# Block-sparse attention and a token mix on one core: edge queries in twelve joined units, two places for the keys, and key copies spread over three engines

## The chip, the cores and the metric

The kernel runs on one core of one Trainium2 chip. The metric is the device time of one execution in microseconds (us). Before the change it was 636.45 us, the median of three runs from 635.98 to 636.53. All parts of the profile below are of one profiled execution, which took 636.82 us; the span from its first to its last instruction was 635.0 us, so 1.8 us lie around the span.

The engines are called as the profile calls them: PE multiplies matrices (PEld loads its stationary operand), DVE is the vector engine, ACT the scalar engine, POOL is GpSimd, and SP issues most of the DMAs. PSUM is the memory that PE writes to, SBUF the main on-chip memory.

## The reference

A block-sparse attention over 4 batches, 8 heads, 768 tokens and 64 channels per head feeds a token mix. Blocks have 32 tokens, so there are 24 of them. A query block sees its own block and the two beside it, the first and the last block, and three sampled blocks; the first and the last query block see everything.

```python
mask = np.abs(blk_i - blk_j) <= window            # window = 1
mask = mask | (blk_i == 0) | (blk_j == 0) | (blk_i == n_blocks - 1) | (blk_j == n_blocks - 1)
for qb in range(n_blocks):
    for kb in sampled_blocks[qb]:
        mask[qb*block:(qb+1)*block, kb*block:(kb+1)*block] = True
scores = np.where(mask, scale * q @ k.T, -1e9)
attn = np.exp(scores - np.max(scores, -1, keepdims=True))
x = (attn / (attn.sum(-1, keepdims=True) + 1e-9)) @ v       # then (batch, 768, 512)

theta = x @ w_theta
y = w_tok_r @ (x * cos(theta)) + w_tok_i @ (x * sin(theta)) # over the tokens
u = x + y
out = u + np.maximum(u @ w_ch, 0.0)
```

The four weights come as 64-bit floats. The kernel decodes them from their two 32-bit words into a high and a low part, and multiplies with both.

## The kernel before

Two stages follow each other: `attention` and `token_mix`. Both run on the same engines, and the last steps of the first overlap the first loads of the second.

**Attention** works on two pairs of batches, one after the other. A pair has 30 units: 8 wide units (the two edge query blocks, once for each batch and half of the heads, against all 768 keys; tiles SW, PW, Tw, XW) and 22 inner units (query blocks 1 to 22 for all heads, against 8 key blocks gathered into a buffer kg). A unit passes through five steps on different engines: scores on PE into a PSUM tile S, the row extremes m on DVE (TENSOR_REDUCE, L291), the exponentials P on ACT (L300, four instructions), eight transposes on PE and their copy from PSUM to pT on ACT (L307, L309), the products with the values on PE (L318, tile X), and the division by the row sums on DVE (L325 to L328), whose result xo is stored to the intermediate xs in HBM. The order is written out by hand: step n of the loop in `attention` issues the scores of unit n+1, the transposes of unit n, the weights of unit n+1 and the values of unit n-1, and around them the work that prepares later units.

That preparation is what the change touches. `gather_k` fills kg for unit n+2 from the pair's keys kb: window and edge blocks on ACT with a scaling of -1/8 (L235), three sampled blocks on DVE at addresses held in registers (L244), which `number_blocks` loads (L224, TENSOR_LOAD). There is one buffer for kb, so the keys of the second pair can be loaded only when the first pair has been gathered (L209). `load_window` loads the neighbouring value rows into one of two buffers va (L260, L263); `gather_v` fetches the sampled value rows into one of three buffers vb with an indirect DMA from POOL's queue (L270). The `Decoder` decodes one third of a piece of 512 weight columns in most steps: `bits` (L67 to L69), `rest` (L75, L77) and `low` (L83, L84) on DVE, `start` and `high` (L63, L80) on ACT. A new raw piece is loaded when `low` has freed its buffer.

**The token mix** runs 48 steps. In each PE computes an angle block (tile h, L517 to L519) and 24 products into y (L555 to L557), later also the output products o (L578 to L580). The last weight, w_ch, is decoded in its first 12 steps, two thirds of a 256-column piece in a step.

Of the kernel before, what the change touches and what calls it, by code (L numbers as in the profile page):

```python
# [19 lines left out]
P = 128  # L20
# [3 lines left out]
VB_BUFS = 3  # L24
Q_AHEAD = 4
Q_BUFS = 3
RAW_AHEAD = 6
# [18 lines left out]
class Piece:  # L46
# [5 lines left out]
    def __init__(self, nc, hi, lo, src, name):  # L52
        self.nc, self.hi, self.lo, self.src, self.name = nc, hi, lo, src, name
        self.f = src.shape[1] // 2
# [10 lines left out]
    def bits(self):  # L65
        nc, a, ai = self.nc, self.a, self.a.bitcast(I32)
        nc.vector.tensor_scalar(a, a, WORD_LO, WORD_HI, op0=ALU.max, op1=ALU.min)  # L67
        nc.vector.tensor_scalar(ai, ai, 4, 1, op0=ALU.logical_shift_left, op1=ALU.logical_shift_right)
        nc.vector.scalar_tensor_tensor(ai, self.raw[:, :, 1], SIGN_BIT, ai, op0=ALU.bitwise_and, op1=ALU.bitwise_or)  # L69
# [12 lines left out]
    def low(self):  # L82
        self.nc.vector.tensor_tensor(self.a, self.a, self.hi.bitcast(F32), op=ALU.subtract)  # L83
        self.nc.vector.tensor_tensor(self.lo, self.a, self.raw[:, :, 0].bitcast(F32), op=ALU.add)  # L84


class Decoder:


    def __init__(self, pieces, pool, queue):  # L90
        self.pieces, self.pool, self.queue = pieces, pool, queue
        self.at = 0
        for piece in pieces[:2]:
            piece.load(pool, queue)

    def left(self):
        return max(3 * len(self.pieces) - self.at, 0)

    def ahead(self, n):

        for k in range(self.at, min(self.at + n, 3 * len(self.pieces))):
            piece = self.pieces[k // 3]
            if k % 3 == 0:
                piece.start()
            elif k % 3 == 2:
                piece.high()

    def go(self, n):
        for k in range(self.at, min(self.at + n, 3 * len(self.pieces))):
            piece = self.pieces[k // 3]  # L110
            (piece.bits, piece.rest, piece.low)[k % 3]()
            if k % 3 == 2 and k // 3 + 2 < len(self.pieces):
                self.pieces[k // 3 + 2].load(self.pool, self.queue)
        self.at += n
# [51 lines left out]
def attention(tc, qT, qE, kT, vr, sampled, xs, ident, pieces, follow):  # L166
# [9 lines left out]
    with ExitStack() as ctx, ExitStack() as early:  # L176
# [5 lines left out]
        vp = ctx.enter_context(tc.tile_pool(name="vp", bufs=2))  # L182
# [4 lines left out]
        ps_t = ctx.enter_context(tc.tile_pool(name="ps_t", bufs=1, space=PSUM))  # L187
        ps_x = ctx.enter_context(tc.tile_pool(name="ps_x", bufs=2, space=PSUM))
# [6 lines left out]
        vas = [cp.tile([P, 1040], F32, name=f"va{x}") for x in range(2)]  # L195
        vbs = [cp.tile([P, 1040], F32, name=f"vb{x}") for x in range(VB_BUFS)]
        kbs, qbs, qes, vws, st, xws, numbers = {}, {}, {}, {}, {}, {}, {}
# [8 lines left out]
        def load_k(bp, b, p0=0, n=4, queue=nc.sync):  # L206
            if (b, p0) == (0, 0):
                kbs[bp] = kp.tile([P, 8, NB, 32], F32, tag="kb", name=f"kb{bp}")
            queue.dma_start(kbs[bp][:, 4 * b + p0 : 4 * b + p0 + n], kT[bp, b][:, p0 : p0 + n])  # L209

        def load_edges(bp):
            raw = ep.tile([P, 512], F32, tag="qw", name=f"qw{bp}")
            nc.sync.dma_start(raw, qE[bp])
            qes[bp] = raw

        def turn_edges(bp):
            t = ep.tile([P, 2, 2, 4, 32], F32, tag="qe", name=f"qe{bp}")
            nc.vector.tensor_scalar(t.rearrange("r z b p f -> r (z b p f)"), qes[bp], -0.125, None, op0=ALU.mult)
            qes[bp] = t

        def number_blocks(bp, i):
            _, numbers[bp, i] = nc.values_load_multi_w_load_instructions(  # L224
                tab.block[0:1, 3 * i : 3 * i + 3], engines=[mybir.EngineType.DVE], min_val=0, max_val=NB - 1,
                skip_runtime_bounds_check_because="Tables clamps the block numbers",
            )

        def gather_k(bp, i):
            kg, kb = kgs[i % 2], kbs[bp]  # L230
            def blocks(b0, n):
                return kb[:, :, b0 : b0 + n, :].rearrange("r g s f -> r s g f")

            def copy(s0, b0, n):
                nc.scalar.activation(kg[:, s0 : s0 + n], blocks(b0, n), AF.Copy, scale=-0.125)  # L235

            if i <= 2:
                copy(3, 0, 1)
                copy(7, NB - 1, 1)
            for b0, n in fresh(i, i <= 2):  # L240
                copy(b0 % 3, b0, n)
            for k, number in enumerate(numbers.pop((bp, i))):
                src = kb[:, :, bass.ds(number, 1), :].rearrange("r g s f -> r s g f")
                nc.vector.tensor_scalar(kg[:, 4 + k : 5 + k], src, -0.125, None, op0=ALU.mult)  # L244
            st[bp, i] = dict(kg=kg)

        def fresh(i, new):

            runs = []
            for blk in range(i - 1 if new else i, i + 2):  # L250
# [5 lines left out]

        def load_window(bp, i):
# [3 lines left out]
            for b0, n in fresh(i, i <= 2):  # L261
                s0 = 32 * (b0 % 3)
                nc.sync.dma_start(va[s0 : s0 + 32 * n], vr[768 * bp + 32 * b0 : 768 * bp + 32 * (b0 + n)])  # L263
            st[bp, i]["va"] = va

        def gather_v(bp, i):
            vb = vbs[i % VB_BUFS]
            if i <= VB_BUFS:
# [7 lines left out]
            st[bp, i]["vb"] = vb  # L276

        def scores(bp, i):

            s = st[bp, i]  # L280
            q = qbs.pop((bp, i))
            kg = s["kg"]
            sc = ps_s.tile([P, 2, 2, 256], F32, tag="S", name=f"S{bp}_{i}")
            for b in range(2):
                for p in range(4):
                    for e in range(2):
                        rows = slice(64 * e, 64 * e + 64)
                        nc.tensor.matmul(sc[32 * p : 32 * p + 32, e, b, :], q[rows, b, p, :], kg[rows, :, 4 * b + p, :], start=True, stop=True)  # L288
            m = wp.tile([P, 2, 2], F32, tag="m", name=f"m{bp}_{i}", bufs=3)
            for e in range(2):  # L290
                nc.vector.tensor_reduce(m[:, e], sc[:, e], axis=AX.X, op=ALU.min)  # L291
            s["S"] = sc, m

        def weights(bp, i):
            s = st[bp, i]
            sc, m = s.pop("S")
            s["P"] = pt = wp.tile([P, 2, 2, 256], F32, tag="P", name=f"P{bp}_{i}")
            for e in range(2):
                for b in range(2):
                    nc.scalar.activation(pt[:, e, b, :], sc[:, e, b, :], AF.Exp, bias=m[:, e, b : b + 1], scale=-1.0)  # L300

        def turned(pts, name):

            n = len(pts)
            t = ps_t.tile([P, 8, 128], F32, tag="T", name=f"T{name}")
            for k, pt in enumerate(pts):
                nc.tensor.transpose(t[:, k, :], pt, ident)  # L307
            out = wp.tile([P, 8, 128], F32, tag="pT", name=f"pT{name}")
            nc.scalar.copy(out[:, :n], t[:, :n])  # L309
            return out  # L310
# [404 lines left out]
```

## Time and profile before

| what | value |
|---|---|
| median of 3 runs | 636.45 us |
| profiled execution, its span | 636.82 us, 635.0 us |
| PE, DVE, ACT, POOL busy | 89%, 73%, 57%, 7% of the span |
| DMA moved | 96.5 MB, 152 GB/s over the span |
| mean granted PE clock | 0.964 |

Busy shares are means over both stages. The stages differ: while attention runs (until about 290 us) DVE, PE and the DMA engines are each busy for 75 to 90% of the time, and in the token mix PE is busy nearly throughout and the DMA engines for a quarter. The parts of the profile that the prediction shows are not repeated here.

### The profile page before, as it was taken

Reading aid. Unit: us, or ns where it says so; the run is one execution under the profiler, and the core shown is the slowest. Engines: PE = TensorE matmul, PEld = TensorE weight load, DVE = VectorE, ACT = ScalarE, POOL = GpSimd, SP = SyncE. Lnnn points to the kernel's source line nnn. Section 1 sums busy time; section 2 is a strip of 40 time slices with the busy share of each in tenths; the row PEclk is TensorE's granted clock in tenths of the full one; section 3 lists DMA queues with packets and bytes.
Section 4 is the critical chain, followed back from the end, with each engine's and each line's share of the span. In section 5 each row is a group of like instructions: output and inputs, shape, how many; then the busy total and the mean of one; then the engine's idle time right before and its main releaser. Section 6 shows DMA issues by size and latency. Waiting matters only on the chain.

```text
span 635.0 us, 19148 instructions
## 1 busy us (share of the span) xinstructions
PE 563.2 (89%) x7808; PEld 483.1 (76%) x7808; DVE 463.5 (73%) x1239; ACT 361.0 (57%) x774; POOL 45.6 (7%) x56
## 2 busy tenths in 40 slices
PE   4987778769887768668999999999999999999997
PEld 1555545545455546547999999999999999999997
DVE  1897978875798878758999697575973767746554
ACT  1586768764587767656667564355642465524520
POOL 0101212211002211110000000000000000000000
PEclk9998989988898999887999999999999999999999
DMA  8859979999778997866542224211241211211002
GB/s 287 259 156 246 275 209 259 258 278 345 219 204 244 251 257 226 221 161 170 139 130 73 64 84 143 69 47 50 80 124 59 70 51 42 80 59 61 27 1 99
DMA packets 79959, 96.52 MB, mean 152 GB/s; under 512 B 5312, under 2 KB 64832, under 8 KB 79488
## 3 DMA queue, kind: packets, MB, share of 16 engines
q1 hardware_dynamic: 73088, 72.99, 39.2%
q0 software_dynamic: 4928, 17.57, 10.7%
q10 hardware_dynamic: 1856, 4.74, 2.1%
q8 instruction: 61, 1.00, 0.7%
q14 instruction: 26, 0.21, 0.1%
HBM read 82.70 MB, written 12.58 MB: 150 GB/s over the span
## 4 chain that ended last, share of the span: by engine, by line
PE 66%; DMA 18%; DVE 8%; issue 4%; ACT 2%; SPq 1%; DVEq 1%; ACTq 0%
PE y L555 10%; PE y L556 10%; PE y L557 10%; DMA va<-in_vr_dram 10%; PE X L318 4%; PE S L288 4%; PE T L307 4%; PE h L519 3%; PE h L518 3%; PE o L578 3%; PE h L517 3%; PE o L580 3%; PE o L579 3%; DMA kb<-in_kT_dram 3%; PE SW L357 2%
## 5 line engine op out<-in xcount | busy, mean ns | idle before, releaser
L300 ACT ACTIVATE P<-S,m 128x256 f32<-128x256 f32 x176 | 69.0, 477 | 15.1 <-DVE m L291 14.9
L307 PEld LDWEIGHTS T<-ident,P 128*128 128x128 f32 x352 | 42.1, 150 | 38.2 <-ACT P L300 25.9
L307 PE MATMUL T<-ident,P 128*128 128x128 f32 x352 | 60.5, 304 | 11.2 <-ACT P L300 6.1
L318 PE MATMUL X<-va,pT 128*32 128x65 f32 (+1 forms) x1408 | 50.3, 233 | 21.9 <-DMA va<-in_vr_dram 18.1
L291 DVE TENSOR_REDUCE m<-S 128x2 f32<-128x512 f32 x88 | 56.7, 686 | 16.7 <-PE S L288 9.8
L309 ACT COPY pT<-T 128x1024 f32<-128x1024 f32 x44 | 44.8, 1018 | 41.5 <-PE T L307 41.4
L288 PE MATMUL S<-kg,q 64*32 64x256 f32 x1408 | 55.1, 404 | 10.9 <-issue 10.9
L555 PE MATMUL y<-w_tok_r_hi,zh 128*128 128x384 f32 x192 | 64.6, 336 | 0.0
L556 PE MATMUL y<-w_tok_r_lo,zh 128*128 128x384 f32 x192 | 64.4, 335 | 0.0
L557 PE MATMUL y<-w_tok_r_hi,zl 128*128 128x384 f32 x192 | 64.3, 335 | 0.0
L556 PE MATMUL y<-w_tok_i_lo,zh 128*128 128x384 f32 x192 | 64.2, 334 | 0.0
L555 PE MATMUL y<-w_tok_i_hi,zh 128*128 128x384 f32 x192 | 64.2, 334 | 0.0
L557 PE MATMUL y<-w_tok_i_hi,zl 128*128 128x384 f32 x192 | 62.7, 334 | 0.0
L270 POOL DMA_INDIRECT vb<-in_vr_dram,rows x44 | 44.1, 1002 | 229.3 <-PE X L318 206.0
L318 PEld LDWEIGHTS X<-va,pT 128*32 128x32 f32 (+1 forms) x1408 | 35.6, 116 | 31.8 <-DMA va<-in_vr_dram 17.8
L517 PE MATMUL h<-w_theta_hi,xTh 128*128 128x256 f32 x192 | 55.8, 290 | 1.9 <-ACT xTh L508 1.9
L519 PE MATMUL h<-w_theta_hi,xTl 128*128 128x256 f32 x192 | 55.6, 290 | 0.5 <-DVE xTl L509 0.5
L518 PE MATMUL h<-w_theta_lo,xTh 128*128 128x256 f32 x192 | 55.3, 288 | 0.0
L318 PE MATMUL X<-vb,pT 128*32 128x65 f32 (+1 forms) x1408 | 49.8, 232 | 5.0 <-issue 5.0
L521 ACT ACTIVATE t<-h,up_int 128x256 f32<-128x256 f32 x48 | 22.7, 473 | 42.7 <-PE h L519 42.0
L528 ACT ACTIVATE cs<-rr 128x256 f32<-128x256 f32 x48 | 20.0, 416 | 45.8 <-DVE rr L526 45.8
L578 PE MATMUL o<-uh,w_ch_hi 128*128 128x384 f32 x128 | 42.5, 336 | 0.9 <-DVE of L584 0.9
(125 smaller groups left out, 1337.2 us busy)
## 6 DMA issues: line engine op xcount, KB each, us to landing
xa<-xs SPq DMA_DIRECT2D x192, 64.0 KB
va<-in_vr_dram SPq DMA_DIRECT2D x30, 260.0 KB
xr<-xs SPq DMA_DIRECT2D x24, 256.0 KB
out_dram<-of SPq DMA_DIRECT2D x32, 192.0 KB
q<-in_qT_dram SPq DMA_DIRECT2D x22, 256.0 KB
xs<-xo SPq DMA_DIRECT2D x44, 128.0 KB
vw<-in_vr_dram SPq DMA_DIRECT2D x6, 780.0 KB
raw_tok_r<-in_w_tok_r_dram SPq DMA_DIRECT2D x9, 512.0 KB
```

Source lines behind the costliest of these rows:

```text
L288: nc.tensor.matmul(sc[32 * p : 32 * p + 32, e, b, :], q[rows, b, p, :], kg[rows, :, 4 * b + p, :], start=True, stop=True)
L291: nc.vector.tensor_reduce(m[:, e], sc[:, e], axis=AX.X, op=ALU.min)
L300: nc.scalar.activation(pt[:, e, b, :], sc[:, e, b, :], AF.Exp, bias=m[:, e, b : b + 1], scale=-1.0)
L307: nc.tensor.transpose(t[:, k, :], pt, ident)
L318: nc.tensor.matmul(x[32 * p : 32 * p + 32, g, :], pt[0:rows, k, 32 * p : 32 * p + 32], v[0:rows, v0 + 65 * p : v0 + 65 * p + 65], start=st ...
L517: nc.tensor.matmul(ps, hi[:, c, :], wh[:, c, :], start=c == 0, stop=False)
L518: nc.tensor.matmul(ps, hi[:, c, :], wl[:, c, :], start=False, stop=False)
L519: nc.tensor.matmul(ps, lo[:, c, :], wh[:, c, :], start=False, stop=c == 3)
L555: nc.tensor.matmul(acc, zh[:, dd], wh[:, j, tt], start=j == 0 and m == 0, stop=False)
L556: nc.tensor.matmul(acc, zh[:, dd], wl[:, j, tt], start=False, stop=False)
L557: nc.tensor.matmul(acc, zl[:, dd], wh[:, j, tt], start=False, stop=j == 5 and m == 1)
L578: nc.tensor.matmul(ps, wh[:, c, :], uh, start=c == 0, stop=False)
```

## The change

The attention stage is rebuilt, and what is tied to it is moved:

- The edge queries become 6 units a pair in place of 8: for each of the two edge blocks (z) and each third of the keys (t, 8 key blocks) one unit for all heads, in the shape of an inner unit. Each has maxima of its own; `join` then rescales the three partial sums to a common maximum and adds them on POOL.
- Keys are not scaled when they are copied. The factor 1/8 goes into the exponential, and DVE makes the negative scaled maxima nm with one more small instruction.
- The two pairs' keys have places of their own. The first pair's keys and its 6 value tiles lie in a place that later holds the second half of the token weights; the second pair's keys are loaded in steps 8, 14 and 20, and its wide value tiles go into the vb buffers, of which there are now four.
- kg is filled by three engines: neighbours and edge blocks by POOL, two sampled blocks by DVE, the third by ACT.
- `low` of the decoder runs on POOL in halves of a piece; token weights are decoded in pieces of 576 columns. w_ch is decoded one whole piece in each of the first 8 steps of the token mix.
- The transposed weights have two PSUM banks of their own and two copies; X has one PSUM buffer where it had two.
- xs is stored with both batches of a pair side by side, 1 KB in a row.

```diff
+    def on_gpsimd(self):
+        if self.lows:
+            k, half = self.lows.pop(0)
+            piece = self.pieces[k]
+            piece.low(piece.nc.gpsimd, half * (piece.f // 2), piece.f // 2)
+            if half == 1:
+                self.load(k + 2)
...
+        def sampled_keys(bp, i, k):
+            src = ks[bp][:, bass.ds(numbers[bp, i][k], 1)].rearrange("r s g f -> r s (g f)")
+            return kgs[i % 2].rearrange("r s g f -> r s (g f)")[:, 4 + k : 5 + k], src
+        def gather_keys(bp, i):
+            for k in range(2):
+                nc.vector.tensor_copy(*sampled_keys(bp, i, k))
+        def gather_key(bp, i):
+            nc.scalar.copy(*sampled_keys(bp, i, 2))
...
+            for s0, b0, n in runs:
+                nc.gpsimd.tensor_copy(kgs[i % 2][:, s0 : s0 + n], ks[bp][:, b0 : b0 + n])
...
-                nc.vector.tensor_reduce(m[:, e], sc[:, e], axis=AX.X, op=ALU.min)
+                nc.vector.tensor_reduce(m[:, 2 * e : 2 * e + 2], sc[:, e], axis=AX.X, op=ALU.max)
+            nm = wp.tile([P, 4], F32, tag="nm", name=f"nm{name(unit)}", bufs=2)
+            nc.vector.tensor_scalar(nm, m, -0.125, None, op0=ALU.mult)
...
-                    nc.scalar.activation(pt[:, e, b, :], sc[:, e, b, :], AF.Exp, bias=m[:, e, b : b + 1], scale=-1.0)
+                    nc.scalar.activation(pt[:, e, b], sc[:, e, b], AF.Exp, bias=nm[:, 2 * e + b : 2 * e + b + 1], scale=0.125)
...
+        def join(bp, z):
+            xw, f = xws[z], mxs[z].rearrange("r t (e b) -> r t b e", e=2)
+            for t in range(3):
+                nc.gpsimd.tensor_tensor(xw[:, t], xw[:, t], f[:, t].unsqueeze(3).to_broadcast([P, 2, 2, 65]), op=ALU.mult)
+            nc.gpsimd.tensor_tensor(xw[:, 0], xw[:, 0], xw[:, 1], op=ALU.add)
+            nc.gpsimd.tensor_tensor(xw[:, 0], xw[:, 0], xw[:, 2], op=ALU.add)
...
+            units += [(bp, "w", (z, t)) for t in range(3) for z in range(2)] + [(bp, i, None) for i in range(1, NB - 1)]
...
+            for n in range(steps):
+                do(n + 1, scores)
+                inner(n + 3, number_blocks)
+                inner(n + 2, gather_keys)
...
+                if decoder.at < min(due, 2 * len(decoder.pieces)):
+                    decoder.on_vector()
+                do(n, turn)
+                do(n - 1, values)
+                do(n, evict)
+                do(n + 1, weights)
+                inner(n + 2, gather_key)
+                decoder.on_scalar()
+                do(n - 1, finish)
+                inner(n + 2, gather_window)
+                inner(n + 1, load_window)
+                inner(n - 1, store)
+                inner(n + 2, gather_values)
...
+                decoder.on_gpsimd()
+                inner(n + 4, load_q)
+                if n in (8, 14, 20):
+                    load_k(1, 8 * ((n - 8) // 6), 8)
...
+                for t, step in enumerate((half - 2, half, half + 2)):
+                    if n == step:
+                        load_wide(1, t)
```

What stands in which order shows only in the built program. The rows below give the line, the instruction, and what it writes and reads; P is the exponentials' tile, its number the query block.

ACT before, in the first pair, from the transposed copy of unit 9 to the weights of unit 11:

```order
L309 COPY pT_9_1435<-T_9_1426 128x1024
L300 ACTIVATE P_10_1437<-S_10_1406,m_10_1423 128x256 x4
L235 ACTIVATE kg_116<-kb_131 128x512
L63 ACTIVATE da_tok_r_1498<-raw_tok_r_1161 128x512
L309 COPY pT_10_1529<-T_10_1520 128x1024
L300 ACTIVATE P_11_1531<-S_11_1500,m_11_1517 128x256 x4
```

ACT in the changed program, the same stretch:

```order
L246 TENSOR_LOAD sb_block
L358 COPY pT_9_1578<-T_9_0_1535 128x512
L358 COPY pT_9_1578<-T_9_1_1536 128x512
L342 ACTIVATE P_10_1581<-S_10_1500,nm_10_1520 128x256 x4
L263 ISA
L263 COPY kg_111<-kv_122 128x256
L63 ACTIVATE da_tok_r_1587<-raw_tok_r_1399 128x576
L246 TENSOR_LOAD sb_block
```

Before, the copy into kg behind the weights of unit 10 is for unit 12, whose scores come after the weights of unit 11. In the changed program the copy behind the weights of unit 10 is for unit 11, whose scores come next on PE.

DVE before, from the row extremes of unit 10 to those of unit 11:

```order
L291 TENSOR_REDUCE m_10_1423<-S_10_1406 128x2 x2
L83 TENSOR_TENSOR da_tok_i_1217<-da_tok_i_1217,w_tok_i_hi 128x512
L84 TENSOR_TENSOR w_tok_i_lo<-da_tok_i_1217,raw_tok_i_880 128x512
L325 TENSOR_SCALAR sm_8_1481<-X_8_1446 128x4
L326 RECIPROCAL sm_8_1481<-sm_8_1481 128x4
L328 TENSOR_TENSOR xo_8_1484<-X_8_1446,sm_8_1481 128x256
L244 ISA
L244 TENSOR_SCALAR kg_116<-kb_131 128x256
...
L224 TENSOR_LOAD sb_block
L291 TENSOR_REDUCE m_11_1517<-S_11_1500 128x2 x2
```

DVE in the changed program, from the maxima of unit 9 to those of unit 10:

```order
L324 TENSOR_REDUCE m_9_1420<-S_9_1403 128x2 x2
L326 TENSOR_SCALAR nm_9_1423<-m_9_1420 128x4
L246 TENSOR_LOAD sb_block
L260 ISA
L260 COPY kg_110<-kv_122 128x256
...
L68 TENSOR_SCALAR da_theta_1289<-da_theta_1289 128x512
L69 TENSOR_SCALAR da_theta_1289<-da_theta_1289 128x512
L70 SCALAR_TENSOR_TENSOR da_theta_1289<-raw_theta_1004,da_theta_1289 128x512
L382 TENSOR_SCALAR sm_7_1491<-X_7_1448 128x4
...
L324 TENSOR_REDUCE m_10_1517<-S_10_1500 128x2 x2
```

The decoder's subtraction and addition (L83, L84) are gone from DVE, the register load stands between nm and the two remaining key copies, and the small instruction nm is new.

POOL in the changed program, two steps of the first pair (before, a step had the one row of the indirect DMA):

```order
L281 COPY kg_110<-kv_122 128x512
L295 DMA vb_115<-in_vr_dram,rows 96x1040
L85 TENSOR_TENSOR da_tok_r_1587<-da_tok_r_1587,w_first 128x288
L86 TENSOR_TENSOR w_first<-da_tok_r_1587,raw_tok_r_1399 128x288
L281 COPY kg_111<-kv_122 128x256 x2
L295 DMA vb_116<-in_vr_dram,rows 96x1040
```

Each step has a copy of the window's fresh keys ahead of the indirect DMA, and behind it, in most steps, one half of `low`.

More of the change, by code (lines that the diff above doesn't have):

```diff
@@ L223, in number_blocks @@
-        def number_blocks(bp, i):
[L224 to L245, printed above, removed]
@@ L622, in token_mix @@
                 turn(k + 3)
-            if 0 < k < 13:
-                decoder.ahead(2)
-                decoder.go(2)
+            if k < len(ch):
+                ch[k].start()
+                ch[k].bits()
+                ch[k].rest()
+                ch[k].high()
+                ch[k].low(nc.vector, 0, 256)
+                if k + 2 < len(ch):
+                    ch[k + 2].load(stage, nc.sync)
             mix(k)
@@ L664, in sparse_attention_then_token_mix, with first_place, second, tok @@
[L664 to L665 removed]
+    def first_place(shape, dtype, name):
+        return const.tile(shape, dtype, tag="place", name=name)
+    rest = []
+    def second():
+        if not rest:
+            rest.append(first_place([P, 2, 9 * 768], F32R, "w_second"))
+        return rest[0]
+    def tok(at):
+        tile_, k = (first, at) if at < 3 else (second(), at - 3)
+        return [tile_[:, x, 768 * k : 768 * k + 768] for x in range(2)]
```

408 lines of the change are left out of this document (209 added, 199 removed).

## The prediction

> **What bounds the kernel now.** I read the page's head and its chain first, then busy time by stage, then the PE timeline for the starts of the stages, then one inner step.
>
> ```profile
> span 635.0 us, 19148 instructions
> PE 66%; DMA 18%; DVE 8%; issue 4%; ACT 2%; SPq 1%; DVEq 1%; ACTq 0%
> core 0: us, PE busy (x) PEld busy (x) DVE busy (x) ACT busy (x) POOL busy (x), PEclk, DMA share, GB/s
> 0.00:38.50 38.50, 29.68 (x458) 14.77 (x459) 20.73 (x60) 16.69 (x24) 4.39 (x15) 1.00 0.81 263
> 38.50:136.10 97.60, 75.82 (x2158) 50.74 (x2153) 82.85 (x218) 73.89 (x151) 18.89 (x18) 0.96 0.88 237
> 136.10:175.20 39.10, 32.57 (x702) 20.17 (x698) 26.08 (x54) 20.53 (x32) 3.65 (x4) 0.88 0.89 287
> 175.20:274.30 99.10, 76.15 (x2167) 52.35 (x2160) 82.06 (x215) 72.27 (x149) 17.71 (x18) 0.93 0.85 229
> 274.30:302.00 27.70, 20.29 (x304) 17.20 (x301) 19.51 (x63) 16.80 (x37) 0.91 (x1) 0.76 0.66 173
> 302.00:635.00 333.00, 328.71 (x2054) 327.90 (x2052) 232.31 (x632) 160.78 (x387) 0.00 (x0) 1.00 0.24 74
> ```
>
> The last 333.0 us are the token mix, with PE busy for 328.7 of them: only its start can move. Before it no engine is full: in the two inner stages DVE has 85 and 83%, the DMA engines 0.88 and 0.85. The cuts come from these PE rows:
>
> ```profile
> 8.45 7.19 PE L357 MATMUL SW<-kb,qe 64*32 64x512 f32 x32 [8.45 <-DMA kb<-in_kT_dram]
> 38.52 0.81 PE L288 MATMUL S<-kg,q 64*32 64x256 f32 x17
> 136.08 1.96 PE L288 MATMUL S<-kg,q 64*32 64x256 f32 x32
> 144.15 1.50 PE L357 MATMUL SW<-kb,qe 64*32 64x512 f32 x16 [3.71 <-DMA kb<-in_kT_dram]
> 175.25 1.09 PE L288 MATMUL S<-kg,q 64*32 64x256 f32 x32
> 178.73 1.09 PE L288 MATMUL S<-kg,q 64*32 64x256 f32 x32
> 274.26 1.09 PE L288 MATMUL S<-kg,q 64*32 64x256 f32 x32
> 302.01 0.52 PE L555 MATMUL y<-w_tok_r_hi,zh 128*128 128x384 f32 x1
> PE X L318 <- DMA va<-in_vr_dram: 18.1, 14, 3.5
> ```
>
> Scores of unit 1 to unit 22 are 21 steps: 97.6/21 = 4.65 us a step in the first pair, 99.0/21 = 4.71 in the second. Between the pairs lie 39.2 us, 8.1 of them until the new keys are there; from the last scores to the first product y 27.7. The last row (us in total, times, longest) shows what stretches inner steps: PE waits for window values.
>
> **The inner step of the changed kernel.** This carries most of the sum. Scores of a unit now wait for the third sampled key, which ACT copies behind the exponentials of the unit just before; these wait for nm, nm for both maxima, and those for that unit's scores. The step is thus a loop through PE, DVE and ACT. Its parts:
>
> ```profile
> 88.05 1.09 PE L288 MATMUL S<-kg,q 64*32 64x256 f32 x11 [3.75 <-issue]
> 89.22 1.29 DVE L291 TENSOR_REDUCE m<-S 128x2 f32<-128x512 f32 x2 [3.31 <-PE S L288]
> 92.03 1.57 ACT L300 ACTIVATE P<-S,m 128x256 f32<-128x256 f32 x4
> 93.47 0.66 ACT L235 ACTIVATE kg<-kb 128x512 f32<-128x512 f32 x1
> 101.91 1.29 DVE L291 TENSOR_REDUCE m<-S 128x2 f32<-128x512 f32 x2 [0.23 <-PE T L307]
> 103.29 1.57 ACT L300 ACTIVATE P<-S,m 128x256 f32<-128x256 f32 x4 [0.39 <-DVE m L291]
> 104.64 0.16 DVE L325 TENSOR_SCALAR sm<-X 128x4 f32<-128x4 f32 x1
> 104.83 0.18 DVE L326 RECIPROCAL sm<-sm 128x4 f32<-128x4 f32 x1
> 105.04 0.43 DVE L328 TENSOR_TENSOR xo<-X,sm 128x256 f32<-128x256 f32 x1
> L542 ACT CAST zh<-cs 128x256 fp32r<-128x256 f32 x48 | 19.4, 405 | 15.0 <-DVE cs L539 14.9
> ```
>
> Scores 1.09; to DVE 89.22-89.14 = 0.08; maxima 1.29; nm 0.20 (a dependent 128x4 instruction starts 0.19 to 0.21 after the one before); to ACT 103.29-103.20 = 0.09; exponentials 1.57; the copy starts 93.60-93.47 = 0.13 before they end and takes 0.40 (as the 128x256 CAST); back to PE 0.08 as to DVE. The sum is **4.67 us**. The transposes and their two copies lie beside the maxima. It was no loop before: there the copy into kg was a unit further ahead.
>
> DVE must also fit into the step:
>
> ```profile
> L224 DVEq TENSOR_LOAD <-sb_block x44: 740/748/996, 33.4 to 264.7; - x44
> L244 DVE TENSOR_SCALAR kg<-kb 128x256 f32 x132 | 30.3, 284 | 0.0
> 103.12 0.42 DVE L67 TENSOR_SCALAR da_tok_i<-da_tok_i 128x512 f32<-128x512 f32 x1
> 103.57 0.43 DVE L68 TENSOR_SCALAR da_tok_i<-da_tok_i 128x512 int32<-128x512 int32 x1
> 104.03 0.69 DVE L69 SCALAR_TENSOR_TENSOR da_tok_i<-raw_tok_i,da_tok_i 128x512 int32<-128x512 int32 x1
> ```
>
> Counted from the start of the scores, nm ends at 2.66. The register load (748 ns) stood behind three long copies and is now behind the short nm, which waits itself: it holds DVE's queue to about 3.35. Two copies end at 3.9 (0.28 each, partly overlapped). The first half of a decode takes 104.64-103.12 = 1.52, for 576 columns 1.7, and xo 0.75: 6.35. The next maxima could start at 4.67+1.17 = 5.84, so such a step is 0.51 longer. The second half (L75, L77: 1.25) ends within 0.06. In a step without decode nothing is late. By the changed order 6 first halves lie among the first pair's 21 steps and 10 among the second's. Gone from DVE are `low` and one key copy; DVE was 3.9 to 4.2 us a step and is now 3.4 to 5.1.
>
> Waits for window values I cost at 0.05 us a step: their load now goes out ahead of the store of xo, and 4.7 us a step leaves two steps, 9.4 us, for load and use. Ends: nothing, and 18.1/42 = 0.43 as now.
>
> So the first pair has 21x4.67 + 6x0.51 + 1 = 102.2 (now 97.6), the second 21x4.67 + 10x0.51 + 0.6 + 1 = 104.8 (now 99.0). Inner steps get slower, not faster.
>
> **The other stages.** Start: at the first stage's rate at full share, 263/0.81 = 325 GB/s, the 1.87 MB that the first scores need now take 5.8 of their 8.45 us. The changed order has 6.15 MB up to the last third of the keys: 2.7+18.9 = 21.6 us. One more wide unit (4), a loop step (4.7) and a cold PE clock (about 1: the 32 SW instructions at 8.45 us took 7.19) lead to inner scores at 32; the joins on POOL, five instructions for each z, hold the next window copies for about 1 us. I take **33.0** (38.5 now; ends 30 and 36).
>
> Between the pairs: second keys loaded long before, so no 8.1 us wait. Seven steps at 3.5 us, the rhythm of 175.25 to 178.73, with 3 for late joins: **27.5** (39.2; ends 24 and 34). The wide value tiles go into vb buffers three steps ahead. POOL's joins are late work for nobody but the window copies behind them.
>
> Last scores to first y: the loads of xr still wait for the last read of the keys, and DVE still stands before xr's transposes, so I keep 27.0 of 27.7.
>
> ```profile
> L77 DVE SCALAR_TENSOR_TENSOR raw_ch<-raw_ch,ds_ch 128x256 f32<-128x256 uint32 x8 | 3.3, 417 | 0.0
> ```
>
> Token mix: seven such instructions a w_ch piece, 2.1 to 2.5 us, now whole in each of the first 8 steps instead of two thirds in 12, and the third to sixth block's transposes stand behind the first products. PE has thetas and two y blocks to go on with. I take +2 (0 to 5). The larger rows of xs and one X buffer (xo ends before the next X by over 1 us) I cost at nothing; were they wrong, one X wait is 0.4.
>
> **Sum**: 33.0 + 102.2 + 27.5 + 104.8 + 27.0 + 335.0 = 629.5 us of span, with the 1.8 around it 631.3 for this execution, which lies 0.4 above the median: **631.0**.
>
> **Rivals.** (1) POOL and DVE take turns at SBUF, and the kernel gets slower. The trace shows half of it:
>
> ```profile
> 92.38 0.91 POOL L270 DMA_INDIRECT vb<-in_vr_dram,rows  x1 [7.76 <-PE X L318]
> 95.46 0.70 DVE L77 SCALAR_TENSOR_TENSOR raw_tok_r<-raw_tok_r,ds_tok_r 128x512 f32<-128x512 uint32 x1
> 95.77 1.17 POOL L270 DMA_INDIRECT vb<-in_vr_dram,rows  x1 [2.48 <-PE X L318]
> masks.py:199 POOL TENSOR_SCALAR_AFFINE_SELECT ident<-ident 128x128 f32<-128x128 f32 x1 | 0.3, 289 | 0.0
> ```
>
> Where a decode instruction of DVE has 0.39 us to go, POOL's 0.91 becomes 1.17, as if it first had to see it end. If DVE waits for POOL in the same way, a first half of decode and the second half of `low` meet in 10 steps of the second pair and two between the pairs, with two POOL instructions of 288 columns each time. Their price: 0.45 as DVE's 256-column ones, up to 0.65 at the AFFINE_SELECT's 2.26 ns a column. That is 12x2x0.45 = 10.8 to 15.6 us where all of it is late: 642 to 647; with some cover 636 to 647, likeliest **641**. It decides from 0.13 us a step on, since 5.5 us spread over 42 steps use up the gain. The Trainium skill says this in SBUF — State Buffer, "Who interferes with whom": the two share a port pair as an exclusive lock, against DVE's two-port modes and its instructions with two SBUF inputs. The trace agrees for POOL waiting; no row shows DVE waiting. By the Trainium skill's GPSIMD Engine Reference, "Elementwise — side-by-side cycle accounting", a two-input POOL instruction of 2048 columns takes 4497 ns; 288 would be 0.63, an estimate within my bounds.
>
> (2) DVE's queue is not held by the register load, and the overruns vanish: minus 8.8; wide steps at 3.1 take 3 more: **619**.
>
> (3) Transfers bound the first inner stage. It moved 237x97.6 = 23.1 MB and now has the second keys (3.1 MB) and a wide value load too, some 26 to 27 MB. At 237/0.88 = 269 GB/s these fit into 102 us; at the 237 reached they take 112: **641**.
>
> (4) The pair change doesn't get cheaper, because the wide values arrive late: the 8 us come back, **639**.
>
> **Chances.** Forecast 0.42 (own range 623 to 636), (1) 0.33, (2) 0.12, (3) 0.07, (4) 0.06. A measurement tells 0.2%, 1.3 us, from no change. Faster: 0.38 of the forecast, (2), and 0.02 of the rest: 0.52. Same: 0.08, from the edges of the forecast, (1) and (4). Slower: 0.40. Range 617 to 647: it leaves out the low part of (2) and the high end of (1).
>
> **What would show it.** Scores to scores in quiet steps without decode: 4.6 to 4.8 us, PE's wait before them released by ACT's copy into kg. Steps with a first half: 5.2, or 6 and more with DVE gaps beside POOL's tensor instructions (1). First inner scores at 32 to 34 us; 27 us between the pairs without a wait for keys; the first y at about 294 us. Wrong it would be if quiet steps ran at 4 us, so that no such loop binds, or if window values were still what PE waits for.

## The result and the profile after

The changed kernel takes 673.75 us, the median of four runs from 671.11 to 677.48, against 636.49 before: a ratio of 1.058, with a 95% interval from 1.052 to 1.064. It was forecast at 631.0 with a range up to 647, so it is slower by 37 us and outside the range. The profiled execution took 673.03 us, its span 671.1.

First the busy time by stage again, cut at the same events: first inner scores, last inner scores of the first pair, first inner scores of the second pair, its last, first y. Columns as before.

```profile
core 0: us, PE busy (x) PEld busy (x) DVE busy (x) ACT busy (x) POOL busy (x), PEclk, DMA share, GB/s
0.00:33.10 33.10, 21.06 (x488) 13.92 (x489) 17.91 (x65) 17.68 (x42) 4.15 (x16) 0.90 0.82 287
33.10:152.00 118.90, 76.99 (x2188) 56.30 (x2190) 80.20 (x202) 68.46 (x160) 63.64 (x86) 0.90 0.79 220
152.00:181.80 29.80, 24.28 (x728) 17.24 (x728) 22.49 (x53) 21.77 (x50) 11.92 (x16) 0.93 0.60 201
181.80:305.60 123.80, 85.74 (x2185) 63.54 (x2186) 104.17 (x221) 74.78 (x167) 81.69 (x102) 0.82 0.77 213
305.60:325.50 19.90, 11.43 (x264) 9.65 (x265) 12.61 (x40) 12.45 (x27) 3.65 (x4) 0.80 0.44 118
325.50:671.00 345.50, 337.52 (x2088) 336.21 (x2088) 238.57 (x651) 164.05 (x392) 0.00 (x0) 0.99 0.25 76
```

| stage | before | forecast | measured | missed by |
|---|---|---|---|---|
| start to first inner scores | 38.5 | 33.0 | 33.1 | +0.1 |
| 21 inner steps, first pair | 97.6 | 102.2 | 118.9 | +16.7 |
| between the pairs | 39.2 | 27.5 | 29.8 | +2.3 |
| 21 inner steps, second pair | 99.0 | 104.8 | 123.8 | +19.0 |
| last scores to the end (27.7 + 333.0 before) | 360.7 | 362.0 | 365.4 | +3.4 |

Almost the whole miss, 35.7 of 41.5 us, lies in the inner steps. DVE's row in the second of these stages is the odd one: 104.17 us busy for 221 instructions, where before 215 took 82.06, although the change took work from DVE.

One quiet step of the first pair, from the timeline of all engines (start, duration, engine, line), and a row of the table of waits:

```profile
82.50 1.10 PE L316 MATMUL S<-kg,q 64*32 64x256 f32 x32 [1.55 <-ACT kg L263]
83.69 1.29 DVE L324 TENSOR_REDUCE m<-S 128x2 f32<-128x512 f32 x2 [1.37 <-PE S L316]
85.09 0.17 DVE L326 TENSOR_SCALAR nm<-m 128x4 f32<-128x4 f32 x1
85.29 1.57 ACT L342 ACTIVATE P<-S,nm 128x256 f32<-128x256 f32 x4
86.74 0.42 ACT L263 COPY kg<-kv 128x256 f32 x1
87.26 1.10 PE L316 MATMUL S<-kg,q 64*32 64x256 f32 x32 [1.59 <-ACT kg L263]
...
PE S L316 <- ACT kg L263: 40.1, 23, 3.5
```

This is the loop that the prediction drew, part by part: scores, maxima, nm, exponentials, key copy, scores. It takes 87.26-82.50 = 4.76 us (forecast 4.67). By the last row (us in total, times, longest) PE's scores wait for that copy more than for anything else. No step of either inner stage is shorter than 4.75.

A step of the second pair in which `low` runs, DVE and POOL in order of time:

```profile
205.57 0.93 DVE L326 TENSOR_SCALAR nm<-m 128x4 f32<-128x4 f32 x1
205.64 0.82 POOL L85 TENSOR_TENSOR da_tok_r<-da_tok_r,w_second 128x288 f32<-128x288 f32 x1
206.41 1.10 DVE L260 COPY kg<-k 128x256 f32 x2
206.54 0.82 POOL L86 TENSOR_TENSOR w_second<-da_tok_r,raw_tok_r 128x288 fp32r<-128x288 f32 x1
207.31 0.67 POOL L281 COPY kg<-k 128x512 f32<-128x512 f32 x1
207.43 0.86 DVE L68 TENSOR_SCALAR da_tok_r<-da_tok_r 128x576 f32<-128x576 f32 x1
```

nm, four columns wide, takes 0.93 in place of 0.17 and ends at 206.50, 0.04 after POOL's instruction. The two key copies end at 207.51 (1.10, where 0.49 is usual), 0.15 after POOL's next; the decode instruction takes 0.86 in place of 0.45 and ends 0.31 after POOL's copy. DVE waits for POOL instruction by instruction, and nm lies on the loop. By groups, for the whole kernel (count, busy time, mean ns of one):

```profile
L260 DVE COPY kg<-k 128x256 f32 x44 | 19.9, 494 | 8.7 <-issue 8.7
L324 DVE TENSOR_REDUCE m<-S 128x2 f32<-128x512 f32 x88 | 56.6, 684 | 27.1 <-PE S L316 27.1
L85 POOL TENSOR_TENSOR da_tok_i<-da_tok_i,w_second 128x288 f32<-128x288 f32 x16 | 16.4, 1026 | 36.6 <-DVE ds_tok_i L76 27.7 <-ACT P L342 8.7
L281 POOL COPY kg<-k 128x256 f32<-128x256 f32 (+2 forms) x33 | 18.9, 589 | 0.7 <-PE S L316 0.7
```

The key copies, SBUF to SBUF, went from 284 to 494 ns in the second pair; the maxima, which read PSUM, stayed at 684 (686 before). To have one number for a stage, I take for each DVE instruction its duration less the tenth percentile of its form (line and shape), and add these up. That **excess** is 0.7 us in each inner stage before, and 9.4 and 22.4 now.

### The profile page after: what moved, and what is told of

Its sections match the earlier page's. It is cut to its first block, busy times and chain, and to the rows that moved or that the text cites. A ratio compares the mean times of both kernels' runs of the same rounds, so it can differ in the third digit from the quotient of the medians.

```text
span 671.1 us, 19726 instructions
## 1 busy us (share of the span) xinstructions
PE 557.0 (83%) x7936; PEld 496.9 (74%) x7936; DVE 475.9 (71%) x1227; ACT 359.2 (54%) x836; POOL 165.0 (25%) x222
## 4 chain that ended last, share of the span: by engine, by line
PE 57%; DVE 15%; DMA 12%; ACT 6%; issue 5%; SPq 2%; POOL 2%; DVEq 1%; ACTq 0%; POOLq 0%
PE y L598 9%; PE y L599 9%; PE y L600 9%; PE S L316 6%; DVE m L324 4%; ACT P L342 3%; PE o L621 3%; PE o L623 3%; PE o L622 3%; PE h L562 3%; PE h L561 3%; PE h L560 3%; PE T L352 2%; DMA out_dram<-of 2%; PE X L374 2%
## 5 line engine op out<-in xcount | busy, mean ns | idle before, releaser
L598 PE MATMUL y<-w_second,zh 128*128 128x384 f32 x288 | 97.1, 337 | 0.0
L599 PE MATMUL y<-w_second,zh 128*128 128x384 f32 x288 | 97.0, 337 | 0.0
L316 PEld LDWEIGHTS S<-kg,q 64*32 64x32 f32 x1408 | 26.7, 111 | 89.1 <-issue 49.2
L600 PE MATMUL y<-w_second,zl 128*128 128x384 f32 x288 | 92.6, 334 | 0.0
L358 ACT COPY pT<-T 128x512 f32<-128x512 f32 x88 | 48.0, 588 | 56.2 <-PE T L352 55.8
L342 ACT ACTIVATE P<-S,nm 128x256 f32<-128x256 f32 x176 | 69.2, 479 | 10.1 <-DVE nm L326 9.9
L352 PEld LDWEIGHTS T<-ident,P 128*128 128x128 f32 x352 | 46.0, 162 | 25.8 <-issue 20.0
L374 PE MATMUL X<-va,pT 128*32 128x65 f32 (+1 forms) x1408 | 52.3, 246 | 9.1 <-DMA va<-in_vr_dram 4.6
L598 PEld LDWEIGHTS y<-w_second,zh 128*128 128x128 f32 x288 | 54.8, 190 | 0.0
L599 PEld LDWEIGHTS y<-w_second,zh 128*128 128x128 f32 x288 | 54.7, 190 | 0.0
L374 PE MATMUL X<-vb,pT 128*32 128x65 f32 (+1 forms) x1408 | 52.2, 243 | 2.1 <-issue 2.1
L600 PEld LDWEIGHTS y<-w_second,zl 128*128 128x128 f32 x288 | 53.7, 188 | 0.0
L571 ACT ACTIVATE cs<-rr 128x256 f32<-128x256 f32 x48 | 19.9, 415 | 44.0 <-DVE rr L569 43.9
```

What stands on the lines that cost most here:

```text
L342: nc.scalar.activation(pt[:, e, b], sc[:, e, b], AF.Exp, bias=nm[:, 2 * e + b : 2 * e + b + 1], scale=0.125)
L352: nc.tensor.transpose(banks[k // 4][:, k % 4], pt[:, (k // 2) % 2, k % 2, 128 * (k // 4) : 128 * (k // 4) + 128], ident)
L358: nc.scalar.copy(out[:, 4 * h : 4 * h + 4], bank)
L374: nc.tensor.matmul(s["X"][32 * p : 32 * p + 32, b, e, :], s["T"][0:rows, 4 * c + 2 * e + b, 32 * p : 32 * p + 32], v[0:rows, v0 : v0 + 65] ...
L598: nc.tensor.matmul(acc, zh[:, dd], wh[:, tt], start=j == 0 and m == 0, stop=False)
L599: nc.tensor.matmul(acc, zh[:, dd], wl[:, tt], start=False, stop=False)
```

## The experiments

Two theories were set against each other: (A) POOL and DVE take turns at SBUF, and (C) the loop alone sets the steps; beside them (B), that POOL's results merely come late. All medians are of 4 to 6 runs, and each ratio is against runs of the kernel before on the same chip.

**POOL work that nobody reads, in the kernel before.**

```diff
+        extra = cp.tile([P, 2, 288], F32, name="extra")
+        nc.gpsimd.memset(extra, 0.0)
...
                 do(n + 2, gather_v)
+                for _ in range(2):
+                    nc.gpsimd.tensor_tensor(extra[:, 0], extra[:, 0], extra[:, 1], op=ALU.add)
```

> The kernel before, with two more GpSimd instructions at the end of each attention step (128x288, both inputs in SBUF, on a tile that nothing else reads). Theory A, POOL and DVE take turns at SBUF: in the changed kernel POOL's 61 us of tensor instructions in the second inner stage go with 22.4 us by which DVE's instructions there exceed their usual durations (0.7 before). At that rate 62 x 2 x 0.8 us of POOL give about 37 us of excess on DVE, mostly in its copies and scalar instructions, and the kernel is 8 to 30 us slower: 645 to 666. Theory B, POOL's work only comes late for those who read it: nobody reads this tile, so DVE's durations stay and the time stays within 1.3 us of 636.5.

658.44 us, ratio 1.033 [1.026, 1.041]; the inner stages went from 97.6 and 99.0 to 106.7 and 103.9. Two groups of the kernel before, then the groups of this one:

```profile
L291 DVE TENSOR_REDUCE m<-S 128x2 f32<-128x512 f32 x88 | 56.7, 686 | 16.7 <-PE S L288 9.8 <-issue 5.3 <-PE T L307 1.6
L77 DVE SCALAR_TENSOR_TENSOR raw_tok_i<-raw_tok_i,ds_tok_i 128x512 f32<-128x512 uint32 x9 | 6.2, 688 | 0.3
...
L246 DVE TENSOR_SCALAR kg<-kb 128x256 f32 x132 | 39.9, 356 | 0.0
L293 DVE TENSOR_REDUCE m<-S 128x2 f32<-128x512 f32 x88 | 56.5, 683 | 6.4 <-issue 4.3 <-PE X L320 1.8 <-PE T L309 0.2
L77 DVE SCALAR_TENSOR_TENSOR raw_tok_i<-raw_tok_i,ds_tok_i 128x512 f32<-128x512 uint32 x9 | 9.2, 1019 | 0.3
```

Key copies 284 to 356 ns, the decoder's product of two SBUF inputs 688 to 1019, maxima as before; excess 19.9, 5.5 (between) and 19.2 us, 45 in all where 37 were expected. Nothing reads the tile, so theory B can't explain this: A is shown, 22 us of time for 124 POOL instructions whose result is not used. The traces agree one by one. From the first to the last inner scores, 73 DVE instructions of this kernel are over 0.1 us longer than the tenth percentile of their form, and all 73 run beside a tensor instruction of POOL; in the changed kernel it is 53 of 53, and in the kernel before there are none. The Trainium skill describes it in SBUF — State Buffer, "Who interferes with whom": copies and scalar instructions in two-port modes, and instructions with two SBUF inputs, block against GpSimd, while a reduction never does. The rows agree in all three; the reductions here read PSUM.

**The same work taken away from the changed kernel.**

```diff
     def low(self, engine, f0, f):
         part = slice(f0, f0 + f)
+        if engine is self.nc.gpsimd:
+            return
```

> The changed kernel without the two GpSimd instructions of low (the low parts of the token weights and theta are not computed; the high parts are read in their place, so PE does the same work). Theory A (turns at SBUF, with low as the larger part of POOL's work): DVE's excess falls from 9.4 and 22.4 us in the two inner stages to about 4 and 6, waits of ACT for nm and of casts for DVE go with it, and the time falls to about 650 (643 to 658). Theory C, the loop through ACT's key copy alone accounts for the slow steps: 4.75 us a step are untouched, DVE's overruns stay, 668 to 674.

657.33 us, with runs from 652.8 to 664.3, 1.031 [1.019, 1.043]: 16.4 less than the changed kernel. Inner stages 114.1 and 112.5 (118.9 and 123.8), excess 2.3 and 2.4. What is left shows the other half. Scores of units 11 to 15 there, from PE's timeline:

```profile
86.79 1.10 PE L318 MATMUL S<-kg,q 64*32 64x256 f32 x32 [1.66 <-ACT kg L265]
91.54 1.10 PE L318 MATMUL S<-kg,q 64*32 64x256 f32 x32 [1.59 <-ACT kg L265]
96.29 1.10 PE L318 MATMUL S<-kg,q 64*32 64x256 f32 x32 [1.59 <-DVE da_tok_r L69]
101.22 1.06 PE L318 MATMUL S<-kg,q 64*32 64x256 f32 x22 [1.76 <-ACT kg L265]
104.81 1.08 PE L318 MATMUL S<-kg,q 64*32 64x256 f32 x10 [2.53 <-issue]
110.28 1.10 PE L318 MATMUL S<-kg,q 64*32 64x256 f32 x32 [0.59 <-issue]
```

A quiet step is 91.54-86.79 = 4.75, as C has it; one step, in which PE stops in the middle of a unit for a reason that the profile doesn't name, takes 110.28-101.22 = 9.06. Set beside the kernel before, the same view:

```profile
58.70 1.09 PE L288 MATMUL S<-kg,q 64*32 64x256 f32 x32
62.09 1.09 PE L288 MATMUL S<-kg,q 64*32 64x256 f32 x32
...
83.25 1.05 PE L288 MATMUL S<-kg,q 64*32 64x256 f32 x21
88.05 1.09 PE L288 MATMUL S<-kg,q 64*32 64x256 f32 x11 [3.75 <-issue]
92.00 1.09 PE L288 MATMUL S<-kg,q 64*32 64x256 f32 x32
```

There too a step has such a stop (92.00-83.25 = 8.75), but a quiet one takes 3.39. The means of 4.65 (first pair) and 4.71 (second) were made of medians of 4.24 and 3.74 and a few long steps. The loop lifts the quiet steps to 4.75, and the long ones stay on top.

Followed along the loop step by step, the second inner stage takes 24.0 us more than 21x4.75 in the changed kernel and 12.7 without `low`. Counted above the quiet step's values, the maxima start late behind the scores by 6.8 and 2.7 us in all, nm is longer by 4.1 and 0.0, the exponentials start late behind nm by 8.0 and 6.8, and the scores themselves, stops of PE included, take 5.2 and 3.2 more. So `low` acts on the loop through DVE, and the late exponentials are for the most part something else. Three of these waits in the changed kernel have a cause that its ACT timeline shows; the first of them:

```profile
217.20 0.74 ACT L63 ACTIVATE da_tok_i<-raw_tok_i 128x576 f32<-128x576 f32 x1 [3.51 <-DMA raw_tok_i<-in_w_tok_i_dram]
217.84 1.05 ACT L358 COPY pT<-T 128x512 f32<-128x512 f32 x2
218.78 1.58 ACT L342 ACTIVATE P<-S,nm 128x256 f32<-128x256 f32 x4
```

nm was ready at 216.54, but ACT stood waiting for a raw piece of weights, and the exponentials came 2.25 us late. The second inner stage has 14.6 us of such waits (before: none in either inner stage). This piece's load was issued at 210.78, 6.4 us ahead of its use; in the second inner stage before, it was 9 us and more. In the changed program the load stands behind the second half of `low`, and a piece is decoded in two steps in place of three. Without `low` on POOL the waits stay (13.7 us), and no run issued these loads earlier.

**The loop cut, POOL left as it is.**

```diff
+                inner(n + 2, gather_key)
                 do(n, evict)
                 do(n + 1, weights)
-                inner(n + 2, gather_key)
```

> The changed kernel with ACT's copy of the third sampled key ahead of the copies of the transposed weights and the exponentials of its step, in place of behind them. Theory C (the loop scores, maxima, exponentials, key copy, scores sets 4.75 us and passes every delay of DVE and ACT on into the step): steps without decode fall to 4.0 to 4.4, the time to 645 to 662. Theory A without the loop (DVE, stretched by POOL, is itself the bound): quiet steps 4.6 or more and 668 to 674.

660.62 us, 1.035 [1.028, 1.043]. Time fell as C expects, but not evenly; its two inner stages, by the columns of the stage view (the profiled execution was the slowest of the four, 665.91):

```profile
31.70:144.20 112.50, 78.55 (x2190) 57.42 (x2191) 78.44 (x199) 67.77 (x157) 62.93 (x85) 0.88 0.82 229
180.50:303.60 123.10, 82.15 (x2184) 58.00 (x2185) 101.38 (x219) 72.50 (x165) 82.17 (x102) 0.89 0.74 214
```

The first inner stage gained 6.4 us, and its fastest steps fell under 4; the second gained 0.7, with the excess at 21.0 and DVE at 101.4 of 123.1 us. In the second pair POOL's `low` holds the steps even without the loop: with `low` left out as well, the next run, the stage takes 105.5. The stage between the pairs became longer (36.4), which no run explains.

**Both together**: `low` left out as above, and the key copy ahead.

> The changed kernel without low on GpSimd (as in no_low, the high parts are read in place of the low ones) and with ACT's third key copy ahead of the exponentials (as in key_first). In no_low quiet steps took 4.75 us to the hundredth, in key_first they fell only in the first pair. Theory A with C (the loop is the floor, turns at SBUF lie on it or hide that it is gone): with both away the floor is scores, maxima, nm, register load, two copies = 3.9 us; quiet steps 3.9 to 4.3, inner stages 95 to 105 and 96 to 106 us, total 632 to 645. Rival (window values or transfers become the floor at once): quiet steps 4.6 or more, total 648 to 658.

648.77 us, 1.016 [1.008, 1.025]; inner stages 108.8 and 105.5. The floor of 3.95 is there in a few steps, but the medians are 4.99 and 4.95, and the time is the rival's. In the table of waits of the second inner stage ACT waits 17.8 us for raw pieces of the weights, up to 3.4 at a time, which fits the rival's transfers; waits for DVE and single stops stand beside them, and no run separates these.

**Neighbouring keys on ACT.**

```diff
-                nc.gpsimd.tensor_copy(kgs[i % 2][:, s0 : s0 + n], ks[bp][:, b0 : b0 + n])
+                nc.scalar.copy(kgs[i % 2][:, s0 : s0 + n], ks[bp][:, b0 : b0 + n])
...
+                inner(n + 2, gather_window)
                 do(n, evict)
...
-                inner(n + 2, gather_window)
```

> The changed kernel with the copies of the neighbouring keys on ACT, ahead of the copies of the transposed weights, in place of POOL. Theory A: DVE's excess falls by a quarter to a third (POOL keeps low and the joins), ACT gets about 0.5 us a step off the loop: 662 to 670. Theory B (POOL late for the scores, through copies that stand behind low and the joins): the waits of PE for these copies, 25 us together by the table of waits, go: 650 to 660. Theory C: no change, 672 to 676.

666.15 us, with runs from 660.3 to 671.4, 1.048 [1.039, 1.057], in A's range; excess 7.8 and 14.7, down by 29%. But in the profiled execution (660.33) the time isn't gained where the excess fell: the first inner stage is 8.9 us shorter with 1.6 us less excess, the second 1.3 shorter with 7.7 less. So this run doesn't tell what the neighbouring keys on POOL cost through DVE. The edit together with `low` left out:

> The changed kernel without low on GpSimd (the high parts are read in place of the low ones) and with the copies of the neighbouring keys on ACT: in the inner steps POOL keeps the indirect DMAs, and the joins at the stages' first steps. Theory A: DVE's excess falls below 1.5 us in each inner stage, and nothing of it is left on the loop; quiet steps stay at 4.7 (the loop), single stalls of PE and late window values remain on top: inner stages 107 to 111 and 108 to 112, total 648 to 656. Rival (something else than POOL's tensor instructions stretches DVE): the excess stays at 2 us or more in each stage.

665.99 us, 1.037 [1.023, 1.050], runs from 655.8 to 668.3, above the expected 648 to 656. The excess was 1.6 and 2.7 us, between the two cases, about half of it beside the joins; why the time isn't below 657 stays open.

**`low` on DVE, at the same place.**

```diff
-            piece.low(piece.nc.gpsimd, half * (piece.f // 2), piece.f // 2)
+            piece.low(piece.nc.vector, half * (piece.f // 2), piece.f // 2)
```

> The changed kernel with the two instructions of low on DVE at the same place of the step, in place of POOL. DVE then has 0.94 us more in most steps of the second pair: by the sum of its instructions a step with a first half is 1.4 us longer than the loop's 4.75, one with a second half 0.9, so about 5.9 us on average in the second inner stage, as with low on POOL (123.75/21 = 5.89): 668 to 677. If turns at SBUF cost more than the work itself: 650 to 665.

669.21 us, 1.053 [1.043, 1.063], in the first range; second inner stage 121.9. So by these medians DVE pays about as much for POOL's two instructions as for doing them itself.

**Three smaller edits**: the register load behind the decoder's instructions, w_ch's decode two steps later, the cast to the high part one step later.

```diff
-                inner(n + 3, number_blocks)
...
                     decoder.on_vector()
+                inner(n + 3, number_blocks)
```

> The changed kernel with the register load of a unit's block numbers behind the decoder's instructions on DVE in place of ahead of the two key copies. The prediction put an overrun of 0.51 us on each of 16 steps, with 0.75 us of this load in it. If it is so, quiet steps stay at 4.75 and the time falls by 5 to 10: 664 to 669. If the load is hidden anyway: 672 to 676.

671.66 us, between the two cases; the inner stages stayed at 119.1 and 124.0, so the load was not what made steps long.

```diff
-            if k < len(ch):
-                ch[k].start()
+            if 2 <= k < len(ch) + 2:
+                ch[k - 2].start()
...
```

> The changed kernel with the decode of w_ch begun in the third step of the token mix in place of the first. In the trace ACT waits 4.6 us for the first raw piece there, and the third block's cast, ready, stands behind it. If that is what makes the third step of the mix 15.6 us long, last scores to the end fall from 365.5 to 359 to 362 us and the time to 668 to 671. If the raw piece is not the reason (the late store of the last units is), 672 to 676.

675.50 us, interval of the ratio 1.049 to 1.068: no gain. But the test failed in itself: the token mix is ordered by the framework's scheduler, and ACT still waited 4.5 us for the first raw piece ahead of the third block's cast.

```diff
-        while self.highs:
+        while self.highs and self.at % 2 == 0:
             self.highs.pop().high()
```

> The changed kernel with ACT's cast to the high part one step later, so that it no longer waits in ACT's queue for DVE's first half of the decode in the same step. In the trace the exponentials start up to 2.25 us behind nm in steps with a first half, 9.6 us in all in the inner stages. If ACT's queue behind that cast is the reason, most of this goes: 664 to 669. If DVE is late there anyhow, 672 to 676.

674.89 us: no gain, and the exponentials were as late behind nm as before. That cast is not the reason.

**All tensor work of the step off POOL, and the loop cut.** `low` on DVE, neighbouring keys on ACT, register load late, and:

```diff
+                inner(n + 2, gather_window)
+                inner(n + 2, gather_key)
                 do(n, evict)
                 do(n + 1, weights)
-                inner(n + 2, gather_key)
```

> The changed kernel with all of the step's tensor work off POOL and the loop cut: low on DVE, the neighbouring keys on ACT, both of ACT's key copies ahead of the transposed copies, the register load behind the decoder's instructions. By the sums (DVE 4.9 us a step in the second pair, 4.3 in the first, stalls of about 9 us a stage on top): inner stages 98 to 106 and 106 to 114, total 636 to 652. If turns at SBUF weren't the main loss, it stays near key_first: 657 or more.

643.77 us, 1.011 [1.003, 1.019] against before: 30 us of the loss of 37 undone. Its two inner stages, by the columns of the stage view:

```profile
33.50:143.50 110.00, 78.51 (x2190) 56.19 (x2194) 81.62 (x223) 80.39 (x193) 24.73 (x28) 0.91 0.83 231
171.20:279.20 108.00, 75.98 (x2197) 53.26 (x2191) 99.12 (x259) 84.04 (x197) 28.42 (x32) 0.95 0.88 247
```

DVE does more here (259 instructions where the changed kernel has 221) in less time (99.1 against 104.2 us busy), with an excess of 3.4. Against before, the start (-5.0) and the stage between the pairs (171.2-143.5 = 27.7, -11.5) keep their gain, and the inner stages still give back 12.4 and 9.0.

**DVE's two key copies ahead of the maxima as well.**

```diff
+                inner(n + 2, gather_keys)
                 do(n + 1, scores)
...
-                inner(n + 2, gather_keys)
```

> As all_off_pool, with DVE's two key copies ahead of the row maxima of the same step, so that no loop through nm is left in the gathering of keys (floor 3.94 us in all_off_pool). If that loop still costs: steps fall to about 3.6 at the fastest, the first inner stage by 4 to 8 us, the second, where DVE is full, by 0 to 3: 632 to 640, level with the kernel before or under it. If single stalls of PE and DVE's own work are all that is left: 641 to 645.

646.34 us, just above the second range, 1.013 [1.007, 1.019]; inner stages 109.0 and 107.6. The fastest steps fell from 3.94 to 3.09 us, but the stages by only 1.0 and 0.3, so that loop wasn't the limit either. No version beat the kernel before.

## Why the prediction was wrong

- **The loop was right.** Its parts sum to 4.67 in the prediction and to 4.75 in the trace, quiet steps wait for ACT's copy, and cutting it brought 13 us. The difference of 0.08 a step is 3.4 us.
- **The step that failed is the sum of the inner stages**, "21x4.67 + 6x0.51 + 1 = 102.2", in three ways. First, 4.67 is a floor, and it was set in place of 4.65, a mean that already held the long steps. The prediction looked at the mean and concluded that a step would change little, though a quiet step of before took 3.4. Without `low` on POOL, the first stage still is 114.1 = 21x4.75 + 14.3. Three steps of 9.06, 7.67 and 6.96 hold 9.4 of these 14.3, where the prediction had 4.1 for overruns and waits.
- **Second, DVE's durations were taken as undisturbed.** That is rival (1), and its mechanism was right; it stood at 0.33 and should have been part of the forecast. The trace of before showed POOL waiting for DVE, and tensor work that then measured 62 us was being added to POOL in the second stage. Its price for `low`, 10.8 to 15.6 us, is about the 16.4 measured, given the scatter of that run, but by luck. A 288-column instruction took 0.79 at least, above the 0.45 to 0.65 of the prediction. (The estimate of 0.63 from the Trainium skill, GPSIMD Engine Reference, "Elementwise — side-by-side cycle accounting", is a fifth too low as well.) The collisions were counted for first halves of decode alone; nm and the key copies meet POOL as well. And the rival's 641 missed too, because it stood on the same sum.
- **Third, ACT was taken as ready when nm is.** The prediction lays the transposes and their two copies beside the maxima and gives the exponentials a delay of 0.09 us. In the second inner stage they started 8.0 us late in all; in three steps, 5.1 us together, because ACT had waited for a raw piece, for which the prediction has no term. In the others the transposes on PE were late.
- The overrun of 0.51 us from the register load was not seen. The load does hold DVE's queue (in the quiet step above the key copies start 0.55 us behind nm), but in most quiet steps without `low` the maxima come at most 0.3 us late, and moving the load changed nothing in the inner stages.
- **Start** (33.0, measured 33.1) and **pair change** (27.5, measured 29.8; 28.0 without `low`) were right: second keys in a place of their own do save the wait. The parts of the pair change were not those of the sum, so its number is partly luck: its quiet steps took 3.1 in place of 3.5, and the last one 7.6, with PE waiting 3.50 for DVE's key copies.
- **Tail and mix** were 362.0, measured 365.4. The first y came earlier than forecast, 19.9 us after the last scores, but PE then ran dry. From the timelines of ACT and PE:

```profile
329.47 0.62 ACT L551 CAST xTh<-r 128x512 fp32r<-128x512 f32 x1 [4.19 <-DVE r L550]
334.68 0.43 ACT L63 ACTIVATE da_ch<-raw_ch 128x256 f32<-128x256 f32 x1 [4.60 <-DMA raw_ch<-in_w_ch_dram]
335.02 0.60 ACT L551 CAST xTh<-r 128x512 fp32r<-128x512 f32 x1
...
347.98 0.46 PE L598 MATMUL y<-w_first,zh 128*128 128x384 f32 x1 [2.40 <-ACT zh L585]
```

  On ACT the cast of a later block stands behind the first piece of w_ch, which waits 4.60 us for its load, and PE waits for z until 347.98. That this order costs the 3.4 us is a reading of these rows and not shown: the run meant to test it didn't change the order.
- Rivals (2), (3) and (4) did not set the time: the overruns did stay away, as in (2), but the time was far from its 619; DMA's share fell (0.88 to 0.79 and 0.85 to 0.77), and no wide value was late. PE's waits for window values fell from 18.1 us to one of 4.6.

Still open is what makes PE stop in the middle of a unit, in both kernels. The places are not random: if all of PE's records (matmuls, weight loads and the semaphore instructions between them) are counted in order, 60 of the 71 stops longer than 1.2 us in the fourteen traces, with nothing that releases them, come at a count that leaves 193 to 195 when divided by 256. So they sit at places of the program that are multiples of 256 instructions apart, whichever matmul (of S, T or X) stands there; why, no run tests. Open is too what holds the inner steps of the last two versions at 5.1 to 5.2 us on average where a few reach 3.9 and 3.1. In their second inner stages ACT still waits 16.3 and 9.4 us for raw pieces.

## What to carry to other kernels

Before work goes to GpSimd to relieve VectorE, list which VectorE instructions will run beside it and what they read: copies and scalar instructions between SBUF tiles, and instructions with two SBUF inputs, were seen to wait until the GpSimd instruction ended, PSUM reductions weren't. Compare a new dependency loop with the median or the fastest step of the old kernel, never with its mean, since rare long steps stay on top of a floor. A short instruction on the loop (nm, 0.17 us) is the worst place for such a wait. And look at what else stands in the queues of the loop's engines: an instruction that waits for a transfer there makes the loop wait with it.

## What the runs showed of the hardware

- A four-column VectorE instruction can take 0.93 us in place of 0.17 when a GpSimd instruction is under way. 124 GpSimd instructions on data that nobody reads cost 22 us in a kernel of 636.
- In the changed kernel 56 reductions from PSUM ran beside a GpSimd tensor instruction and took 685 ns on average; the other 54 took 683.
- On GpSimd a two-input instruction took 0.73 us at 256 columns and 0.79 at 288 (least of each form); a copy of 512 columns took 0.61 and one of 256 0.39 (tenth percentiles).
- On VectorE the product of two SBUF inputs went from 688 to 1019 ns beside GpSimd, the reduction from PSUM from 686 to 683.
